# The last tile's up stage as 49 small products instead of 26 larger ones, with their weight sums made in tiles two and three

## The chip, the cores and the metric

The kernel runs on one core of one Trainium2 chip. The metric is the device time in microseconds (us) of one execution, the median over several. A core has five engines that run at once, each through its own list of instructions in order, and that wait for each other by semaphores: TensorE (PE in the profile; PEld is its weight load), VectorE (DVE), ScalarE (ACT), GpSimd (POOL) and SyncE (SP), which here only issues transfers. TensorE writes to PSUM banks, which VectorE and ScalarE read out; the working memory is SBUF. DMA transfers are issued from SP, ACT and POOL queues and run on 16 DMA engines. In a row such as `SPq`, `ACTq` or `PEq` the letter q marks the engine's sequencer: an issue of a transfer or a wait.

## The reference, cut to what matters

```python
# attention (8 batches, 8 heads, 576 positions, 64 wide), a retention without softmax
scores = scale * np.matmul(q, k.transpose(0, 1, 3, 2))
ret = scores * Dmat          # Dmat[i, j] = gamma_h ** (i - j) for i >= j, else 0
attn = np.matmul(ret, v)
x = attn.transpose(0, 2, 1, 3).reshape(4608, 512)
# gated feed-forward: 512 -> 1536 -> 512
g = x @ w_gate
silu = g * (1.0 / (1.0 + np.exp(-g)))
out = (silu * (x @ w_val)) @ w_out
```

All inputs and outputs are float32 (the weights come as float64 and are rounded in the kernel).

## The kernel before, in words

The 4608 tokens are worked on in five tiles: tile 0 has 512 tokens and plain products, tiles 1 to 4 have 1024 each. A tile of 1024 has an **up stage** (x times `w_gate` and `w_val`, SiLU, product, result `hid`) and a **down stage** (`hid` times `w_out`). The attention of the tokens that come next is cut into ticks that are merged between the products of both stages; tile 4 has none left. `up_step`, `down_step` and `merge` write the order of all engines by hand (`manual_schedule`), so each engine's list is the order of the Python calls.

A down or up stage does not make the 32 block products of a 4x2 by 2x4 block product but 26, after the tables `UP` and `DOWN`: every product is of a sum of blocks of x (or `hid`) with a sum of blocks of the weights, and the results are sums of products. The hidden width of 1536 is cut into three quarters (`qd`, `NQ` = 3), each with 26 products in the up stage. An up product is four matmuls of 128x128 weights with 256 tokens: gate and value side by side in one bank, two halves of the contraction each. A float32 matmul shows as two records in the profile, so a product has eight. The four banks A, B, C, E are handed out by `bank` in the order in which they came to rest; `reads` empties them: copies on ScalarE (L1058), sums with a bank on VectorE (L1061), sums without a bank on GpSimd (L1061 POOL), into 12 `part` places, and `result` makes the SiLU on ScalarE (L1145) and the product on VectorE or GpSimd (L1148 to L1152). `down_step` stores outputs from `part` places to memory on SP (L1182).

The sums of weights are made once, in tile 1, on GpSimd (`w_sums`, L910 and L1095) with negations on ScalarE (`negated`, L1085). They take turns in five `extra` places, and some are made in place in `w_up`, over weights that no longer serve. Each operand is stored to memory when it is used, on ScalarE's queue (`up_ops`, L1128); a place can be used again only when its store is done. In tiles 2 to 4 the operands come back through a ring of eight places of 768 columns, one fetch on SP (`fetch`, L1022) as each product is done, eight products ahead. The sums of x are made by `x_sums`: eight on VectorE in the last four steps of the down stage before, the others on GpSimd in the first quarter of the up stage.

Three things set the order around the change: SP's list (operand fetches, output stores, attention loads; each waits in turn), ScalarE's list (bank copies, SiLUs, negations and, in tile 1, operand stores), and VectorE's list (bank sums, products, attention). The lines that move the work:

```python
    turn = [5, 4, 1, 6, 7, 2, 0, 3]                    # L1015: ring place of fetch m is turn[m % 8]
    nc.sync.dma_start(out=ring[:, turn[m % 8], 0 : src.shape[-1]], in_=src)      # L1022
    nc.scalar.dma_start(out=up_ops[qd][i].rearrange("p (g x) -> p g x", g=2), in_=w)   # L1128, tile 1
    at = 2 * (i - (N - 1 - X_FIRST // 2))              # down_step: x sums of the next tile, steps 21 to 24
```

The last three lines of the table `DOWN` matter at the hand-over to tile 4: they end in `out 1 0 ... out 2 9`, in `out 6 2` and in `add 4 b 4, out 0 4`, where the second number of an `out` is the part that is stored. The first lines of `UP` copy their banks into parts 0 and 1, then 2 and 3, then 4 and 5.

## Time and profile before

| what | value |
|---|---|
| median of 3 runs | 1043.55 us (1042.9 to 1045.37) |
| profiled execution, first to last instruction (its span) | 1037.2 us; no other time of this execution is given |
| median of the runs less that span | 6.35 us |
| mean granted TensorE clock | 0.998 |
| tile 1, up and down | 173 to 318, 318 to 400 us |
| tile 2, up and down | 400 to 545, 545 to 621 us |
| tile 3, up and down | 621 to 762, 762 to 831.5 us |
| tile 4, up and down | 831.5 to 966.2, 966.2 to 1037.2 us |
| DMA traffic | 199.12 MB, mean 192 GB/s |
| operand fetch, up (256 KB) and down (384 KB) | 2.6 and 3.8 us from issue to landing |
| operand store, up (256 KB, ScalarE's queue) | 3.7 us from issue to landing |

How to read it: the page gives each engine's busy time as a share of the span, the chain of work that ended last, and groups of instructions by line with tile names (`rest`, `arena`, `x_odd` and `io` are large SBUF tiles that hold several things; `rest` holds the parts). A row "A <- B: total, times, longest" is idle time of A that ended when B was done. A windows row gives, for a stretch of time, the busy us of TensorE, weight load, VectorE, ScalarE and GpSimd, the granted clock, the busy share of the 16 DMA engines, and GB/s. A timeline row gives start, duration, engine, line, operation, output and input, and in brackets how long the engine had been idle and what ended it.

### The profile page before, as it was taken

What the parts mean: (1) busy time and instruction counts of PE and PEld (TensorE: products, weight loads), DVE (VectorE), ACT (ScalarE), POOL (GpSimd) and SP (SyncE); (2) the same over time, 40 slices, a digit from 0 to 9 for tenths busy, and PEclk for the clock granted to TensorE, in tenths of its full rate; (3) what the DMA queues carried; (4) which work ended last, traced back from release to release, by engine and by line L of the source; (5) the groups of instructions that cost most, each with busy time, mean ns of one, the idle gap of its engine ahead of it and who ended that gap; (6) DMA issues with size and microseconds to landing.
All of it is one profiled execution on the core that took longest, in us unless ns stands there. A gap on an engine that the chain in (4) does not pass through costs nothing.

```text
span 1037.2 us, 21564 instructions
## 1 busy us (share of the span) xinstructions
PE 1023.1 (99%) x8440; PEld 846.0 (82%) x8440; DVE 633.2 (61%) x1070; ACT 299.6 (29%) x653; POOL 419.9 (40%) x369
## 2 busy tenths in 40 slices
PE   6999999999999999999999999999999999999998
PEld 5654555888888888888888888888888888888887
DVE  4488878676768667446458685435465644344644
ACT  3566433253544222222322103223211022231110
POOL 3401265867564236522134057222242583222425
PEclk9999999999999999999999999999999999999999
DMA  9999877777679887674686686555554465555653
GB/s 240 258 279 263 200 218 269 204 205 191 196 194 265 211 244 220 177 197 133 188 231 173 176 208 208 153 142 153 159 171 148 143 196 153 153 153 160 182 163 100
DMA packets 307244, 199.12 MB, mean 192 GB/s; under 512 B 215944, under 2 KB 251784, under 8 KB 307144
## 3 DMA queue, kind: packets, MB, share of 16 engines
q1 hardware_dynamic: 275720, 161.17, 58.2%
q10 hardware_dynamic: 30784, 36.18, 10.4%
q8 instruction: 67, 1.10, 0.5%
q0 software_dynamic: 640, 0.39, 0.2%
q14 instruction: 33, 0.27, 0.1%
HBM read 157.58 MB, written 40.11 MB: 191 GB/s over the span
## 4 chain that ended last, share of the span: by engine, by line
PE 93%; DMA 3%; DVE 1%; ACT 1%; issue 1%; SPq 1%; POOL 0%; DVEq 0%; ACTq 0%; POOLq 0%
PE bankC L1124 13%; PE bankE L1124 13%; PE bankB L1124 13%; PE bankA L1124 13%; PE bankB L1173 7%; PE bankC L1173 7%; PE bankE L1173 7%; PE bankA L1173 7%; PE outer L556 2%; PE bankA L877 2%; PE bankB L877 1%; PE bankE L877 1%; PE outer L583 1%; PE inner L597 1%; PE inner L567 1%; PE bankC L877 1%
## 5 line engine op out<-in xcount | busy, mean ns | idle before, releaser
L1061 POOL TENSOR_TENSOR rest<-rest 128x512 f32<-128x512 f32 x65 | 91.7, 1415 | 234.3 <-DVE rest L1061 212.8
L1145 ACT ACTIVATE io<-rest 128x256 f32<-128x256 f32 x180 | 75.0, 416 | 305.4 <-DVE rest L1061 262.4
L1124 PE MATMUL bankC<-rest,arena 128*128 128x256 f32 x544 | 129.0, 380 | 0.0
L1124 PE MATMUL bankA<-rest,arena 128*128 128x256 f32 x544 | 128.7, 379 | 0.0
L910 POOL TENSOR_TENSOR arena<-arena 128x512 f32<-128x512 f32 (+1 forms) x72 | 110.6, 1549 | 37.3 <-DMA up<-arena 26.5
L1124 PE MATMUL bankB<-rest,arena 128*128 128x256 f32 x512 | 121.2, 380 | 0.5 <-DMA arena<-up 0.5
L1124 PE MATMUL bankE<-rest,arena 128*128 128x256 f32 x512 | 121.4, 380 | 0.1
L1152 POOL TENSOR_TENSOR arena<-rest,io 128x256 f32<-128x256 f32 x72 | 51.9, 726 | 167.7 <-ACT io L1145 167.7
L1124 PEld LDWEIGHTS bankA<-rest,arena 128*128 128x128 f32 x544 | 103.2, 190 | 14.5 <-issue 0.5
L1124 PEld LDWEIGHTS bankC<-rest,arena 128*128 128x128 f32 x544 | 102.9, 190 | 14.4 <-POOL arena L910 0.3
L1124 PEld LDWEIGHTS bankB<-rest,arena 128*128 128x128 f32 x512 | 97.0, 190 | 14.0 <-issue 0.8
L1124 PEld LDWEIGHTS bankE<-rest,arena 128*128 128x128 f32 x512 | 97.0, 190 | 13.7 <-DVE rest L1061 0.5
L910 POOL TENSOR_TENSOR rest<-rest 128x256 f32<-128x256 f32 (+1 forms) x69 | 68.9, 1020 | 71.8 <-DMA dn<-rest 35.3
L1061 DVE TENSOR_TENSOR rest<-bankB,rest 128x512 f32<-128x512 f32 x72 | 48.9, 687 | 67.1 <-PE bankB L1124 52.5
L1061 DVE TENSOR_TENSOR rest<-bankC,rest 128x512 f32<-128x512 f32 x72 | 48.9, 687 | 65.5 <-PE bankC L1124 46.9
L1061 DVE TENSOR_TENSOR rest<-bankA,rest 128x512 f32<-128x512 f32 x72 | 48.9, 687 | 61.2 <-PE bankA L1124 45.1
L1061 DVE TENSOR_TENSOR rest<-bankE,rest 128x512 f32<-128x512 f32 x71 | 48.2, 687 | 60.5 <-PE bankE L1124 47.1
L1148 DVE SCALAR_TENSOR_TENSOR arena<-rest,io 128x256 f32<-128x256 f32 x84 | 56.7, 676 | 10.8 <-ACT io L1145 10.8
L1173 PE MATMUL bankC<-arena 128*128 128x256 f32 x252 | 58.3, 380 | 0.1
L1173 PE MATMUL bankB<-arena 128*128 128x256 f32 x252 | 58.2, 381 | 0.0
L1173 PE MATMUL bankA<-arena 128*128 128x256 f32 x252 | 57.9, 379 | 0.0
L1173 PE MATMUL bankE<-arena 128*128 128x256 f32 x252 | 57.9, 379 | 0.0
(204 smaller groups left out, 1626.1 us busy)
## 6 DMA issues: line engine op xcount, KB each, us to landing
arena<-up SPq DMA_DIRECT2D x234, 256.0 KB, 2.6
arena<-dn SPq DMA_DIRECT2D x104, 384.0 KB, 3.8
up<-arena ACTq DMA_DIRECT2D x78, 256.0 KB, 3.7
dn<-rest SPq DMA_DIRECT2D x78, 128.0 KB, 1.8
out_dram<-rest SPq DMA_DIRECT2D x31, 256.0 KB, 3.9
qk<-in_q_dram SPq DMA_DIRECT2D x108, 72.0 KB, 2.6
qk<-in_k_dram SPq DMA_DIRECT2D x108, 72.0 KB, 2.7
rest<-in_moe_w_out_dram ACTq DMA_DIRECT2D x6, 1024.0 KB
```

Source lines behind the costliest of these rows:

```text
L556: m = nc.tensor.matmul(value(i, hl, c), s["v"][rows, at], ret[rows, c % 2 if whole(i) else hl, c // 2], start=start, stop=start, skip_grou ...
L567: nc.tensor.matmul(z[half[hl], r, c], s["kn"][chunk(i, hl, 2 * c + r)], s["v"][rows, at], start=True, stop=True, skip_group_check=True)
L583: nc.tensor.matmul(xr[half[hl]] if c + 1 == NC else value(i, hl, c), state[half[hl], c, :], s["qT"][half[hl], ts(c, L)], start=False, stop ...
L597: nc.tensor.matmul(sc[chunk(i, hl, 2 * c + r)[0], r if whole(i) else hl, c], kT[half[hl], at], qT[half[hl], at], start=True, stop=True, sk ...
L877: nc.tensor.matmul(bank, w, xs[0][:, c, :], start=(c == 0), stop=(c == HP - 1))
L910: eng.tensor_tensor(out=dst, in0=srcs[0], in1=srcs[1], op=ALU.add if op[0] == "add" else ALU.subtract)
L1061: eng.tensor_tensor(out=at(op[1]), in0=at(op[2]), in1=at(op[3]), op=ALU.add if op[0] == "add" else ALU.subtract)
L1124: m = nc.tensor.matmul(b[:, gv * TB : (gv + 1) * TB], w[:, gv, ts(c, P)], rhs[:, c, :], start=(opens and gv == 0 and c == 0), stop=(c == 1 ...
L1145: nc.scalar.activation(out=s, in_=src[:, 0:TB], func=AF.Silu, scale=-1.0 if negative else 1.0)
L1148: return lambda: nc.vector.scalar_tensor_tensor(out=dst, in0=src[:, TB : 2 * TB], scalar=-1.0, in1=s, op0=ALU.mult, op1=ALU.mult)
L1152: nc.gpsimd.tensor_tensor(out=dst, in0=src[:, TB : 2 * TB], in1=s, op=ALU.mult)
L1173: nc.tensor.matmul(b[:, m * TB : (m + 1) * TB], lhs[:, qd, ts(m, P)], w[:, qd], start=(opens and qd == 0 and m == 0), stop=(qd == NQ - 1), ...
```

## The change

In tile 4 (`FINE`) the up stage is replaced by `fine_up`: for each quarter a form with seven products (a 2x2 by 2x2 block product) is applied twice, 49 products for each quarter. A product contracts 128 instead of 2 x 128 and is two matmuls. Seven outer sets (in the order 1, 2, 6, 7, 4, 5, 3) hold seven inner products each. Inner sums are partly made by adding up in a bank: product 1 opens a bank, 6, 7 and 4 add to it, and ScalarE copies the bank between them; 5 and then 3 share another, 2 has its own. VectorE makes the other inner sums and all outer ones, in four held parts, eight temporary ones and four kept places.

The weight operands of this form need other sums. In tile 1 the raw weights of each quarter are stored to memory (`w_raw`), twice 1 MB, at the quarter's first step. Six weight rounds, three in tile 2's up stage and three in tile 3's, load 1 MB of them back into the third quarter's place of `hid`, which is free then, make twelve sums and store seven operand sets (`fine_ops`), on ScalarE's queue. Tile 4 fetches one outer set (917 KB) at a time into three places. Fetches have places of two sizes, and the down operands of tiles 3 and 4 take other ring places. The x sums of tile 4 are made by VectorE in steps 17 to 20 of tile 3's down stage, by GpSimd in steps 21 to 24 and in the first two outer sets.

```diff
+FINE = (4,)
+FINE_ORDER = (1, 2, 6, 7, 4, 5, 3)
+FINE_SETS = {1: 0, 2: 1, 7: 2, 3: 3, 5: 4, 6: 5, 4: 6}
...
+    w_raw = [[dr.tile([P, 2048], F32, name=f"raw{qd}_{g}") for g in range(2)] for qd in range(NQ)]
+    fine_ops = [dr.tile([P, 2 * 7 * 896], F32, name=f"fine{qd}") for qd in range(NQ)]
...
-    fetches = [("dn", 1, i) for i in range(N)]
-    for n in range(2, NTILE):
-        fetches += [("up", qd, i) for qd in range(NQ) for i in range(N)] + [("dn", n, i) for i in range(N)]
-    fetched = [0]
+    fetches = []
+    def queued(what, a, i, slot=None):
+        if what == "fine":
+            lo, width = len([f for f in fetches if f[0] == "fine"]) % 3 * 1792, 1792
+        else:
+            lo = 768 * (turn[len(fetches) % 8] if slot is None else slot)
+            width = 512 if what == "up" else 768
+        fetches.append((what, a, i, lo, width))
+    for n in range(1, NTILE):
+        if n in FINE:
+            for qd in range(NQ):
+                for o in FINE_ORDER:
+                    queued("fine", qd, FINE_SETS[o])
+        elif n > 1:
+            for qd in range(NQ):
+                for i in range(N):
+                    queued("up", qd, i)
+        for i in range(N):
+            if n in FINE:
+                queued("dn", n, i, (i + 7) % 8)
+            else:
+                queued("dn", n, i, (i + 6) % 8 if n + 1 in FINE else None)
+    fetched, used = [0], [0]
...
+        while fetched[0] < len(fetches):
+            lo, width = fetches[fetched[0]][3:]
+            if any(f[3] < lo + width and lo < f[3] + f[4] for f in fetches[used[0] : fetched[0]]):
+                return
+            fetch_one()
...
+        if busy and i == 0:
+            for g in range(2):
+                nc.scalar.dma_start(out=w_raw[qd][g], in_=w_up[:, qd, g].rearrange("p h k x -> p (h k x)"))
+        if n > 1:
+            for f in rounds.pop((n, qd, i), ()):
+                f()
...
+        if n + 1 in FINE:
+            for f in fine_early.pop((n + 1, i), ()):
+                f()
+        elif 0 <= at < X_FIRST and n + 1 < NTILE:
...
+    def weight_round(qd, g, engines):
...
+        fresh4 = [hid[:, 2].rearrange("p h t x -> p (h t x)")[:, 3584:4096].rearrange("p (n y) -> p n y", n=2),
+                  rest[:, last_at : last_at + 512].rearrange("p (n y) -> p n y", n=2),
+                  operands.rearrange("p (s y) -> p s y", y=768)[:, 0:2, 512:768]]
+        fresh3 = raw_flat[:, 0:1152].rearrange("p (s i x) -> p s i x", s=3, i=3)
...
+        def begin():
+            nc.sync.dma_start(out=raw_flat, in_=w_raw[qd][g])
+        def first():
+            combine(e0, t1, quarter(1, 0), quarter(0, 0), -1)
+            combine(e0, quarter(1, 0), quarter(1, 1), quarter(1, 0), -1)
+        def second():
+            combine(e0, t2, quarter(1, 1), t1, -1)
+            combine(e0, t4, quarter(0, 1), t2, -1)
+        def inner(eng, z, new):
+            return [lambda: (combine(eng, new(0), z(0, 1), z(0, 0), -1), combine(eng, z(0, 1), z(1, 1), z(0, 1), -1)),
+                    lambda: (combine(eng, new(1), z(1, 1), new(0), -1), combine(eng, new(2), z(1, 0), new(1), -1))]
+        def store4():
+            for n in range(2):
+                for k in range(2):
+                    nc.scalar.dma_start(out=to[:, 2 * n + k, 0:512].rearrange("p (m x) -> p m x", m=2), in_=quarter(n, k))
+            for i in range(3):
+                for n in range(2):
+                    nc.scalar.dma_start(out=to[:, 2 * n : 2 * n + 2, 512 + i * P : 512 + (i + 1) * P],
+                                        in_=fresh4[i][:, n].rearrange("p (k x) -> p k x", k=2))
+        def store3():
+            nc.scalar.dma_start(out=to[:, 4:7, 0:512], in_=mid.rearrange("p (s x) -> p s x", s=3))
+            nc.scalar.dma_start(out=to[:, 4:7, 512:896], in_=raw_flat[:, 0:1152].rearrange("p (s x) -> p s x", s=3))
+        return [begin, None, first, second, *inner(e1, z4, lambda i: fresh4[i].rearrange("p n (k x) -> p n k x", k=2)), None, store4, None,
+                *inner(e2, z3, lambda i: fresh3[:, :, i]), None, store3]
+    def plan_rounds():
+        V, G = nc.vector, nc.gpsimd
+        order = [(qd, g) for qd in range(NQ) for g in range(2)]
+        at = [(2, 0, 8), (2, 1, 0), (2, 1, 13), (3, 0, 8), (3, 1, 0), (3, 1, 13)]
+        for (qd, g), (n, stage, i) in zip(order, at, strict=True):
+            for d, f in enumerate(weight_round(qd, g, (V, G, V) if stage else (V, V, V))):
+                if f is not None:
+                    rounds.setdefault((n, stage, i + d), []).append(f)
...
+        def outer_sums(eng):
+            return [lambda: combine(eng, sets[5], sets[7], sets[4], 1),
+                    lambda: combine(eng, sets[6], sets[5], sets[1], -1),
+                    lambda: combine(eng, sets[7], sets[1], sets[7], -1),
+                    lambda: combine(eng, sets[3], sets[2], sets[6], -1)]
+        def inner_sums(o, eng):
+            a, (s1, s2, s4) = sets[o], inner[o]
+            return [lambda: combine(eng, s1, a[:, 0, 1], a[:, 1, 1], 1),
+                    lambda: combine(eng, s2, s1, a[:, 0, 0], -1),
+                    lambda: combine(eng, a[:, 0, 1], a[:, 0, 0], a[:, 0, 1], -1),
+                    lambda: combine(eng, s4, a[:, 1, 0], s2, -1)]
...
+        late = [f for o in FINE_ORDER[3:] for f in inner_sums(o, nc.gpsimd)]
+        held = part[0:4]
+        spot = {11: 0, 12: 1, 21: 2, 22: 3}
+        final = {2: (0, 0), 3: (0, 1), 4: (1, 0), 5: (1, 1)}
+        def temps(k):
+            return dict(zip(("p1", "p5", "u2", "u3"), part[4 + 4 * (k % 2) : 8 + 4 * (k % 2)]))
...
+        home = {11: "p1", 12: "u2", 22: "p5", 21: "u3"}
+        def bank_of(k, i):
+            if i in (1, 6, 7, 4):
+                return banks[k % 2]
+            return banks[2 + (k + (i == 2)) % 2]
+        def product(k, i):
+            qd, o = seq[k]
+            _, _, _, lo, width = fetches[base + k]
+            w = operands[:, lo : lo + width].rearrange("p (g i x) -> p g i x", g=2, i=7)[:, :, PLACE[i]]
+            b = bank_of(k, i)
+            opens = i in (1, 2, 5)
+            for g in range(2):
+                nc.tensor.matmul(b[:, g * TB : (g + 1) * TB], w[:, g], x(o, i),
+                                 start=(opens and g == 0), stop=True, skip_group_check=True)
+        def finish(k, c):
+            qd, o = seq[k]
+            (T, H), (t, h) = final[o], divmod(c - 11, 10)
+            src = temps(k)[home[c]]
+            s = io[:, (silus[0] % 4) * TB : (silus[0] % 4 + 1) * TB]
+            silus[0] += 1
+            nc.scalar.activation(out=s, in_=src[:, 0:TB], func=AF.Silu)
+            nc.gpsimd.tensor_tensor(out=hid[:, qd, 2 * H + h, 2 * T + t], in0=src[:, TB : 2 * TB], in1=s, op=ALU.mult)
+        def outer(k, c, src):
+            o = seq[k][1]
+            r, at = held[spot[c]], temps(k)[home[c]]
+            if o == 2 or o == 3:
+                combine(nc.vector, at, src, r, 1)
+            elif o == 6:
+                combine(nc.vector, r, src, r, 1)
+            elif o == 7:
+                combine(nc.vector, kept(k, c), src, r, 1)
+            elif o == 4:
+                combine(nc.vector, at, src, kept(k, c), 1)
+            elif o == 5:
+                combine(nc.vector, r, src, r, 1)
+                combine(nc.vector, at, src, kept(k, c), 1)
+        def made(k, c, a, b):
+            o = seq[k][1]
+            to = held[spot[c]] if o == 1 else temps(k)[home[c]]
+            combine(nc.vector, to, a, b, 1)
+            if o != 1:
+                outer(k, c, to)
+        def done(k, c):
+            if 0 <= k < K and seq[k][1] in final:
+                finish(k, c)
+        def step(k, r):
+            own, last = 0 <= k < K, 0 < k
+            t = temps(k)
+            if own and r == 0:
+                product(k, 1)
+                nc.scalar.copy(out=t["p1"], in_=bank_of(k, 1))
+            if own and r == 1:
+                product(k, 5)
+                nc.scalar.copy(out=t["p5"], in_=bank_of(k, 5))
+            if last and r == 2:
+                product(k - 1, 4)
+                used[0] += 1
+                fetch()
+            if own and r == 3:
+                product(k, 6)
+                nc.scalar.copy(out=t["u2"], in_=bank_of(k, 6))
+            if own and r == 4:
+                product(k, 2)
+            if own and r == 5:
+                product(k, 3)
+            if own and r == 6:
+                product(k, 7)
+                nc.scalar.copy(out=t["u3"], in_=bank_of(k, 7))
+            if late and own:
+                for _ in range(2):
+                    if late:
+                        late.pop(0)()
+            if r == 0 and last:
+                done(k - 1, 12)
+            if r == 1 and last:
+                before = temps(k - 1)
+                made(k - 1, 22, before["u3"], before["p5"])
+                done(k - 1, 22)
+            if r == 2 and last:
+                if seq[k - 1][1] == 1:
+                    nc.scalar.copy(out=held[spot[21]], in_=bank_of(k - 1, 4))
+                else:
+                    outer(k - 1, 21, bank_of(k - 1, 4))
+            if r == 3 and last:
+                done(k - 1, 21)
+            if own and r == 4:
+                made(k, 11, bank_of(k, 2), t["p1"])
+            if own and r == 5:
+                made(k, 12, bank_of(k, 3), t["u2"])
+            if own and r == 6:
+                done(k, 11)
+        return [lambda k=k, r=r: step(k, r) for k in range(K) for r in range(7)] + [lambda r=r: step(K, r) for r in range(4)]
-        ups = [lambda qd=qd, i=i: up_step(n, qd, i) for qd in range(NQ) for i in range(N)]
+        ups = fine_up(n) if n in FINE else [lambda qd=qd, i=i: up_step(n, qd, i) for qd in range(NQ) for i in range(N)]
```

## The prediction

> **What bounds the kernel now.** I read the busy shares and the chain first, then the stages, then what stands around the places that the change touches.
>
> ```profile
> PE 1023.1 (99%) x8440; PEld 846.0 (82%) x8440; DVE 633.2 (61%) x1070; ACT 299.6 (29%) x653; POOL 419.9 (40%) x369
> PE 93%; DMA 3%; DVE 1%; ACT 1%; issue 1%; SPq 1%; POOL 0%; DVEq 0%; ACTq 0%; POOLq 0%
> ```
>
> TensorE is the bound, and from 10 us on nearly nothing else is. So fewer matmul records are worth their time, and every wait that reaches TensorE is lost whole. The windows by stage (TensorE, weight load, VectorE, ScalarE, GpSimd busy, clock, DMA share, GB/s) are the up stages of tiles 1, 2, 3 and 4, then a stretch of tile 2 and two short ones that show what the DMA engines reach:
>
> ```profile
> 173.00:318.00 145.00, 144.88 (x1228) 126.09 (x1227) 103.29 (x172) 61.86 (x136) 96.58 (x73) 1.00 0.74 207
> 400.00:545.00 145.00, 144.54 (x1169) 126.71 (x1164) 75.93 (x145) 39.31 (x87) 49.61 (x49) 1.00 0.67 188
> 621.00:762.00 141.00, 141.00 (x1002) 124.19 (x996) 69.35 (x119) 36.97 (x81) 52.83 (x51) 1.00 0.59 169
> 831.50:966.20 134.70, 134.70 (x626) 118.58 (x625) 56.83 (x88) 34.41 (x74) 49.69 (x49) 1.00 0.59 165
> ...
> 431.00:476.00 45.00, 45.00 (x460) 39.50 (x459) 21.66 (x42) 13.43 (x30) 9.07 (x11) 1.00 0.60 166
> 333.50:338.50 5.00, 5.00 (x25) 4.41 (x24) 4.06 (x6) 1.34 (x4) 0.00 (x0) 1.00 1.02 367
> ```
>
> Tile 4's up stage is TensorE without a gap: 134.7 us for 26 x 3 products of eight records, 0.216 us a record, 1.727 us a product ("step" below). In 333.5 to 338.5 us all 16 DMA engines are full at 367 GB/s. The SP queue of tile 2 and the chain after it show how far the operand ring carries:
>
> ```profile
> 402.36 10.68 SPq L1022 DMA_DIRECT2D arena<-up  x7
> 414.91 1.96 SPq L306 DMA_DIRECT2D qk<-in_q_dram  x4
> 416.91 3.08 SPq L306 DMA_DIRECT2D qk<-in_k_dram  x4
> ...
> 422.86 6.42 SPq L1022 DMA_DIRECT2D arena<-up  x9
> ```
> ```profile
> 422.86 3.97 DMA arena<-up
> 426.83 0.14 issue
> 426.97 1.97 PE bankB L1124 x8
> ```
>
> SP stopped fetching operands from 413.0 to 422.9 us while attention loads stood ahead; the next operand landed at 426.8, and TensorE waited 0.5 us for it. About 10 us without a fetch is all that the eight ring places carry. Last, tile 1's waits on its own stores, and the hand-over from tile 3's down stage to tile 4:
>
> ```profile
> POOL arena L910 <- DMA up<-arena: 26.5, 10, 8.1
> ACT arena L1085 <- DMA up<-arena: 16.5, 10, 2.6
> ```
> ```profile
> 833.53 0.68 DVE L1061 TENSOR_TENSOR rest<-bankC,rest 128x512 f32<-128x512 f32 x1
> 834.23 0.37 SPq L1182 DMA_DIRECT2D out_dram<-rest  x1
> 837.03 1.07 ACT L1058 COPY rest<-bankB 128x512 f32<-128x512 f32 x2 [0.25 <-DMA out_dram<-rest]
> ```
>
> The last output of tile 3's down stage is stored from part 4; the store is issued at 834.23 and a copy into part 4 can only start at 837.03, 5.5 us into tile 4.
>
> **The change, part by part.** The sum is made against the profiled span, 1037.2 us; the median of the runs, 1043.55, is 6.35 us more, and I add that at the end. 0.3% (3.1 us) is about what a measurement of this kernel tells from none.
>
> *TensorE, tile 4.* 147 products of two matmuls, each two records, are 588 records for 624: 36 x 0.216 = 7.8 us less. This is the whole gain.
>
> *Start of tile 4.* The first product's copy now goes to part 4 (before, part 0). Product 6, third in line, waits for it. Nominally it starts 2 x 0.863 us after the stage, at 833.3. The store of part 4 can be issued about 2 us earlier (eight VectorE x sums leave that spot), but SP holds it behind a 0.92 MB operand fetch (0.92/367 = 2.5 us). It lands between 835.2 (issue at 832.4 plus the 2.8 us seen) and 838.5; with a copy of 0.59 us product 6 starts 2.5 to 5.8 us late. I take 5, as the fetch does stand ahead.
>
> *VectorE and ScalarE, tile 4.* VectorE gets 49 sums a quarter, 147 x 0.69 = 101 us of 127. Outer product 5 has 11 of them, and back to back they start 0.61 us apart: 6.8 us in a window of 7 x 0.863 = 6.04. The backlog reaches TensorE through ScalarE, which waits on each SiLU's input with the bank copies behind it: 0 to 1.5 us, three times; I take 0.5 each. At the stage's end product 4 of the last set follows its copy with no product between: 0.16 drain + 0.59 + wake-up, 1 us. Tile 4: -7.8 + 5 + 1.5 + 1 = 0, between -5 and +5. Its x sums move too: four VectorE and twelve GpSimd ones into steps 17 to 24 of the down stage (GpSimd idles 4.28 us there), 16 GpSimd ones into its first two sets; they are first needed by the fourth set, so I cost them at nothing, with the start's range as cover.
>
> *Tile 1.* Each quarter's first step puts 2 x 1.05 MB of raw weights into the ScalarE queue ahead of the operand stores. Stores take 262 KB a step, 152 GB/s; with the trace's 207 GB/s the engines have 160 GB/s to spare, so the 2.1 MB (5.7 us at 367) needs 13 us to be worked off. GpSimd and ScalarE already wait for these stores (42 us in all). The store of slot 11 (step 3) lands some 4 to 6 us later; ScalarE negates that slot at step 4 with SiLUs behind it, and TensorE needs the result at step 8. The store normally lands near 8.7 us, the negation 0.63 and a GpSimd sum 1.35 make 10.7, and the need is at 13.8: 3 us of slack. 0 to 5 us a quarter, I take 2.5, 7.5 in all.
>
> *A weight round* (six; three in tile 2's up stage, three in tile 3's, from steps 8 of quarter 0, 0 and 13 of quarter 1, over 13 steps each). Per round: one 1.05 MB load on SP; 12 sums of 128x512 or 128x384, all VectorE's in quarter 0, and eight VectorE's (0.6 to 1.1 us) and four GpSimd's (1.35) in quarter 1; 12 stores of 3.21 MB on ScalarE's queue, whose issue takes 0.32 to 0.55 each there, ten of them in one step, 4.5 us in which ScalarE copies no bank.
> The load lands 2.9 us (at 367 GB/s) and about 1.6 us of fixed time after its issue; VectorE asks two steps (3.45 us) on, so it stands about 1 us, then carries 5.5 to 8 us of sums over four to eight steps. The last sums overwrite the raw quarters, so they wait for the first MB of stores: ready at about 13.5 us, and at what a tile-2 stretch leaves (367 - 166 = 201 GB/s) 5.2 us, plus 1.6: 20.3 against VectorE's arrival at 15.6. Behind the waiting sum stand the bank sums; TensorE reuses a bank three or four products later, so about 3.5 to 5.2 us of a VectorE stop are free. Cost of a first or second round: 0 to 5 us, I take 2.5 (lag and ScalarE's 4.5 us come on top of the stop).
> *The third round* starts one step after the second ends. Its load goes into the place that the second's last store is still reading. That store (1.34 MB, issued near 22.5 us from the second round's start, behind the rest of 1.79 MB) ends near 22.5 + 6.7 + 1.6 = 30.8; the load stood first on SP at 22.5. So SP, and behind the load every operand fetch, is held 8.3 us, close to the 10 that the ring carries. The load lands at 35.3; VectorE asked at step 15, 25.9: 9.4 us, less 5.2 of banks, plus the two sums ahead of the bank (1.3) and the bank's own 0.69: 6.2 us of TensorE, and the attention step that falls on the same place (VectorE 13.4 of 16 us busy after it) lengthens the way back: 8. Ends: 2 (stores at the full 367) and 13 (no bank slack, operands late too).
> Tile 2: 2.5 + 2.5 + 8 = 13. Tile 3: 12, as its traffic is 20 GB/s less.
>
> *DMA in all.* Over the second and third round: 8.5 MB of rounds and 166 GB/s x 45 us = 7.5 MB, 356 GB/s against 367. By the row it just fits; with the 305 GB/s of 330 to 340 us it would be 52.4 us for 45, 7 us more, inside the third round's 13.
>
> The Trainium skill's page "DMA: Bandwidth & Descriptors" (Where 436 GB/s comes from) puts the limit between HBM and SBUF at about 358 GB/s for a core. The row above, 367 over 5 us, stands a little over that; by the page the two rounds would need 44.7 of 45 us, so page and row give the same close fit. The page speaks against the change in another section (Issuing engines are not separate DMA queues): giving the stores to ScalarE's queue buys no bandwidth.
>
> *Sum.* 0 + 7.5 + 13 + 12 = +32.5: span 1069.7, time 1076.
>
> **The rivals.**
> *All hidden (faster).* One mechanism decides: the third round's load released in time. If its wait and the stores drain so fast that VectorE stands under 5.2 us, banks cover it; the first two rounds and tile 1 are under their slack, and -7.8 + 2.5 to 5 at the start + 1 is left: about 1040. For: TensorE missed only 0.5 us in 145 with 10 us of SP gone. Against: 1.34 MB must end in 4.1 us, 327 GB/s beside 166 of other traffic. It turns when the waits in tiles 1 to 3 sum under some 3 us.
> *Small loss.* Bank slack and ring hold except in the third rounds at 2 to 4 us each, tile 1 hidden: +6 to +16, about 1054.
> *VectorE bounds tile 4.* Of its 147 sums 63 read a bank and 84 SBUF alone. Those SBUF sums took 682 to 697 ns where GpSimd was idle, 1129 in the mean of a group that ran beside it. All at 1.1: 63 x 0.69 + 84 x 1.1 = 136 us, 9 us over TensorE: 1085. Against: GpSimd has only 48 products of 0.72 us and 16 short sums in 127 us.
> The page "SBUF — State Buffer" (SBUF: two separate sides) calls the port pair shared by the two an exclusive lock for a whole instruction. If every one of those 48 us of GpSimd fell on a VectorE sum, an estimate by that rule is 101 + 48 = 149 us, 22 over TensorE; the rows with GpSimd two thirds busy (a 128x256 product 805 ns, against 589 in tile 4) show a third more, not a full block.
> *DMA saturates everything.* Stores at 305 GB/s, tile 1 at 5 us a quarter, third rounds at 13, the others at 5: +15 + 26 + 20 + 5 = +66, 1109.
>
> **How the numbers follow.** The sum as worked out 0.50; the two larger cases 0.16 together; small loss 0.22; all hidden 0.08; nothing measurable 0.04. The likeliest's own range is 1063 to 1092. Leaving out all hidden and the top of the largest, the 8 in 10 range is 1046 to 1104. Slower by over 0.3% 0.88, within 0.04, faster 0.08.
>
> **What would show it.** The up stage of tile 4 near 127 to 137 us, with a ScalarE copy in its first 8 us waiting on an output store; VectorE waits on the raw load of 1 us in the first rounds and 6 to 12 us in the third ones, with SP standing on the last weight store; TensorE gaps there; slot sums of tile 1 waiting longer on stores at each quarter's start. I am wrong if the third load is released before 27 us of the second round's start, or if TensorE's idle time in tiles 2 and 3 stays under 3 us.

## The result and the profile after

The changed kernel takes 1110.85 us (median of 4 runs, 1106.28 to 1113.6) where the kernel before, run beside it, takes 1043.22: a ratio of 1.065, 95% interval 1.062 to 1.0681. The direction of the forecast was right and its size was not: +32.5 us were forecast and +67.6 came, 6.85 us above the upper end of the range. Of one kernel below, with the raw loads early, the profiled run took 1548.71 us at a mean clock of 0.654 where its other three took 1116.6 to 1121.88; its time is that of the three, and its profile is read only for who waits for whom.

First the page of the changed kernel, its busy line and its chain:

```profile
PE 1040.9 (94%) x8404; PEld 850.4 (76%) x8404; DVE 724.1 (65%) x1182; ACT 328.5 (30%) x713; POOL 456.7 (41%) x412
...
PE 55%; DVE 8%; DMA 6%; POOL 2%; issue 2%; ACT 1%; SPq 1%; ACTq 0%; DVEq 0%; POOLq 0%
```

The 36 matmul records less are there (8404 for 8440), yet TensorE is busy 17.8 us longer, and its share of the chain falls from 93% to 55%. The windows of the up stages of tiles 1 to 4 (span, then busy time of TensorE, weight load, VectorE, ScalarE, GpSimd, the granted clock, DMA share, GB/s):

```profile
178.50:331.40 152.90, 148.50 (x1238) 128.77 (x1237) 107.60 (x176) 61.58 (x138) 96.13 (x73) 0.99 0.83 245
411.20:591.00 179.80, 156.26 (x1169) 133.08 (x1170) 96.03 (x172) 38.67 (x87) 61.09 (x58) 0.92 0.74 222
668.10:824.30 156.20, 146.36 (x897) 126.39 (x898) 91.32 (x145) 36.34 (x81) 64.04 (x59) 0.96 0.71 223
893.40:1039.30 145.90, 130.94 (x590) 111.95 (x589) 104.06 (x145) 65.08 (x132) 55.73 (x69) 0.96 0.44 142
```

Before, the four stages took 146.7, 145.2, 139.6 and 134.7 us, from the first product of each to the first of the next stage (the windows shown before the result end up to 2.6 us away from these borders). So tile 1 lost 6.2 us, tile 2 34.6, tile 3 16.6, tile 4 11.2, and 1.5 more in its down stage; the other down stages are as before, and TensorE came to tile 1 4.6 us later, which varies from run to run (173 to 179 us in the profiles below). These make up the 74.7 us between the two profiled spans, 1111.9 and 1037.2. No stage has its DMA engines full on average (shares of 0.44 to 0.83), though short stretches do: 1.04 from 450 to 455 us, while the first round's stores run. The clock is no longer 1.00 everywhere: in tile 2 it is 0.92 on average, and TensorE's busy time there, 156.26 us for 1169 records, was 144.54 before for as many.

Tile 2's first round on the timeline (start, duration, engine, line, operation, and in brackets the idle time before it and what ended it):

```profile
425.70 1.96 SPq L310 DMA_DIRECT2D qk<-in_q_dram  x4
...
433.02 0.55 SPq L321 DMA_DIRECT2D v<-in_v_dram  x1
...
434.13 0.43 SPq L1269 DMA_DIRECT2D arena<-raw  x1
...
440.52 1.42 DVE L1250 TENSOR_TENSOR arena<-arena 128x512 f32<-128x512 f32 x2 [11.13 <-DMA arena<-raw]
...
445.63 3.75 PE L1166 MATMUL bankC<-rest,arena 128*128 128x256 f32 x8 [6.61 <-DVE rest L1097]
449.18 2.54 PE L1166 MATMUL bankA<-rest,arena 128*128 128x256 f32 x8
451.55 1.89 PE L1166 MATMUL bankB<-rest,arena 128*128 128x256 f32 x8
```

The raw load (L1269) stands behind 8.4 us of attention loads (and one operand fetch) on SP, and VectorE can start 6.4 us after its issue. VectorE, which asks for it two steps after its place in the order, stands 11.1 us with the bank sums behind it, and TensorE 6.6. Then come the rows that the forecast had no term for: the next two products take 3.75 and 2.54 us where 1.89 is the rule. The second round goes the same way (7.3 us of attention loads, VectorE stands 12.8 us, TensorE 7.1). The third round of tile 3, with what SP, VectorE and TensorE show:

```profile
751.67 0.32 SPq L1269 DMA_DIRECT2D arena<-raw  x1
...
756.71 1.42 DVE L1250 TENSOR_TENSOR arena<-arena 128x512 f32<-128x512 f32 x2 [5.83 <-DMA arena<-raw]
...
758.79 3.78 PE L1166 MATMUL bankA<-x_odd,arena 128*128 128x256 f32 x8 [4.38 <-DVE rest L1097]
```

The waits that the rounds add, as totals (in all, times, longest):

```profile
DVE arena L1250 <- DMA arena<-raw: 37.9, 6, 12.8
ACT io L1187 <- DMA fine<-arena: 19.1, 3, 6.7
SPq L1053 <- DMA fine<-arena: 17.9, 11, 3.3
SPq L1269 <- DMA fine<-arena: 13.1, 2, 7.8
```

The first is the one forecast. The second, with two more such waits that end on `fine<-rest`, is ScalarE issuing ten stores in one step (5.8 to 7.7 us in which it empties no bank). The last two are SP standing on stores that ScalarE issued; only the last of them was forecast. At last the start of tile 4:

```profile
896.29 0.53 SPq L1053 DMA_DIRECT2D arena<-fine  x1
896.91 1.08 SPq L1224 DMA_DIRECT2D out_dram<-rest  x2
...
904.01 0.59 ACT L1435 COPY rest<-bankA 128x512 f32<-128x512 f32 x1 [22.84 <-DMA out_dram<-rest]
...
904.65 2.08 PE L1389 MATMUL bankA<-rest,arena 128*128 128x256 f32 x4 [8.17 <-ACT rest L1435]
906.52 1.70 PE L1389 MATMUL bankE<-rest,arena 128*128 128x256 f32 x4
908.05 1.03 PE L1389 MATMUL bankC<-rest,arena 128*128 128x256 f32 x4
```

The first copy of the stage waits on the output store out of part 4, which SP issued behind the operand fetch, and TensorE stands 8.2 us; two slow products follow here too.

### The profile page after: what moved, and what is told of

It reads as the page before. It is cut to its first block, busy times and chain, and to the rows that moved or that the text cites. A ratio compares the mean times of both kernels' runs of the same rounds, so it can differ in the third digit from the quotient of the medians.

```text
span 1111.9 us, 21722 instructions
## 1 busy us (share of the span) xinstructions
PE 1040.9 (94%) x8404; PEld 850.4 (76%) x8404; DVE 724.1 (65%) x1182; ACT 328.5 (30%) x713; POOL 456.7 (41%) x412
## 4 chain that ended last, share of the span: by engine, by line
PE 55%; DVE 8%; DMA 6%; POOL 2%; issue 2%; ACT 1%; SPq 1%; ACTq 0%; DVEq 0%; POOLq 0%
PE bankC L1215 6%; PE bankA L1215 6%; PE bankE L1215 6%; PE bankC L1166 6%; PE bankB L1215 5%; PE bankA L1166 5%; PE bankE L1166 5%; PE bankB L1166 5%; DVE rest L1250 3%; PE bankA L1389 3%; PE bankB L1389 3%; DMA arena<-raw 2%; DMA fine<-arena 2%; DVE arena L1250 2%; PE bankE L1389 2%
## 5 line engine op out<-in xcount | busy, mean ns | idle before, releaser
L1187 ACT ACTIVATE io<-rest 128x256 f32<-128x256 f32 x135 | 55.1, 415 | 269.0 <-DVE rest L1097 179.8
L914 POOL TENSOR_TENSOR arena<-arena 128x512 f32<-128x512 f32 (+1 forms) x72 | 110.9, 1552 | 50.2 <-DMA up<-arena 39.2
L1166 PE MATMUL bankC<-rest,arena 128*128 128x256 f32 x392 | 97.6, 394 | 9.4 <-DVE rest L1097 7.1
L1166 PE MATMUL bankA<-rest,arena 128*128 128x256 f32 x376 | 95.1, 398 | 10.3 <-DVE rest L1097 7.1
L1166 PE MATMUL bankE<-rest,arena 128*128 128x256 f32 x360 | 89.1, 392 | 12.0 <-DVE rest L1097 9.6
L1166 PEld LDWEIGHTS bankC<-rest,arena 128*128 128x128 f32 x392 | 76.8, 198 | 22.5 <-issue 10.1
L1166 PEld LDWEIGHTS bankA<-rest,arena 128*128 128x128 f32 x376 | 74.6, 200 | 23.4 <-DVE rest L1097 7.9
L1166 PE MATMUL bankB<-rest,arena 128*128 128x256 f32 x360 | 86.6, 384 | 1.6 <-DVE rest L1097 1.2
L1166 PEld LDWEIGHTS bankE<-rest,arena 128*128 128x128 f32 x360 | 69.9, 196 | 23.6 <-DVE rest L1097 10.8
L1194 POOL TENSOR_TENSOR arena<-rest,io 128x256 f32<-128x256 f32 x48 | 34.8, 732 | 125.3 <-ACT io L1187 125.3
L1166 PEld LDWEIGHTS bankB<-rest,arena 128*128 128x128 f32 x360 | 68.8, 192 | 12.3 <-DVE rest L1097 1.6
L1250 DVE TENSOR_TENSOR arena<-arena 128x512 f32<-128x512 f32 (+1 forms) x52 | 39.5, 766 | 42.7 <-DMA arena<-raw 37.9
L1250 DVE TENSOR_TENSOR rest<-rest 128x512 f32<-128x512 f32 (+1 forms) x67 | 55.4, 842 | 4.3 <-ACT rest L1452 2.7
```

The costliest lines, as they stand in the source:

```text
L914: eng.tensor_tensor(out=dst, in0=srcs[0], in1=srcs[1], op=ALU.add if op[0] == "add" else ALU.subtract)
L1166: m = nc.tensor.matmul(b[:, gv * TB : (gv + 1) * TB], w[:, gv, ts(c, P)], rhs[:, c, :], start=(opens and gv == 0 and c == 0), stop=(c == 1 ...
L1187: nc.scalar.activation(out=s, in_=src[:, 0:TB], func=AF.Silu, scale=-1.0 if negative else 1.0)
L1194: nc.gpsimd.tensor_tensor(out=dst, in0=src[:, TB : 2 * TB], in1=s, op=ALU.mult)
L1250: eng.tensor_tensor(out=out, in0=a, in1=b, op=ALU.add if sign > 0 else ALU.subtract)
```

## The experiments

The theories, as the expectations name them: **A**, the forecast's own (VectorE stands on a late raw load, with the bank sums behind it); **B**, ScalarE's bank copies come late behind its store issues; **C**, the DMA engines are full; **D**, SP's operand loads are held by ScalarE's list; **E**, GpSimd becomes what is waited for, where it gets the work; **F**, the rounds' work is too much wherever it stands; **H**, half clock after a long stop. Times of up stages in us, with TensorE's stops in brackets where they matter:

| kernel | time | ratio to before, 95% | tile 1 | tile 2 | tile 3 | tile 4 |
|---|---|---|---|---|---|---|
| before | 1043.22 | | 146.7 | 145.2 | 139.6 | 134.7 |
| changed | 1110.85 | 1.062 to 1.0681 | 152.9 | 179.8 (23.5) | 156.2 (9.8) | 145.9 (15.0) |
| no rounds | 1063.49, one run | | 152.8 | 145.0 | 139.6 | 146.9 |
| tile 4's form alone | 1053.48 | 1.0085 to 1.0146 | 146.8 | 144.8 | 139.6 | 145.5 (14.4) |
| the same, other parts first | 1046.92 | 1.0032 to 1.0075 | 146.9 | 145.2 | 139.6 | 138.6 (8.7) |
| raw loads early | 1118.73 | 1.07 to 1.079 | | | | |
| stores only | 1089.71 | 1.0385 to 1.0539 | 152.3 | 176.2 (24.1) | 140.5 (0.7) | 146.7 |
| no stores | 1089.55 | 1.0411 to 1.0509 | 153.4 | 168.2 (17.1) | 149.7 (6.1) | 146.6 |
| rounds 16 steps apart | 1114.68 | 1.0645 to 1.0758 | 152.4 | 173.6 (19.8) | 165.9 (17.5) | 147.3 |
| stores only, GpSimd's queue | 1074.14 | 1.0285 to 1.0356 | 150.8 | 155.1 (6.7) | 143.8 (3.7) | 145.9 |
| stores on GpSimd's queue | 1120.83 | 1.073 to 1.0807 | 153.0 | 186.4 (28.4) | 160.7 (14.2) | 146.0 |
| stores and loads there | 1113.31 | 1.0642 to 1.0752 | 153.0 | 174.9 (18.9) | 166.5 (20.1) | 147.3 |
| and 16 apart, other parts | 1116.92 | 1.0667 to 1.0765 | 152.3 | 180.4 (23.4) | 169.2 (19.8) | 139.8 |
| stretched rounds | 1090.68 | 1.0426 to 1.0508 | 154.7 | 176.6 (24.6) | 146.4 (4.5) | 139.9 |
| and loads on GpSimd's queue | 1092.12 | 1.0439 to 1.0542 | 152.4 | 177.1 (22.9) | 146.5 (5.4) | 138.2 |
| and stores on GpSimd's queue | 1096.69 | 1.0484 to 1.0579 | 150.8 | 169.0 (16.1) | 161.2 (13.1) | 138.7 |

**What each part of the change costs.** First the rounds were left out, with tile 4 taking its weights from another input, then the raw stores of tile 1 too:

```diff
-    plan_rounds()
-            src = fine_ops[a].rearrange(...)
+            src = q[a]...
```
```diff
-        if busy and i == 0:
-            for g in range(2):
-                nc.scalar.dma_start(out=w_raw[qd][g], in_=...)
```

> The changed kernel without the six weight rounds: no loads of raw weights, no sums, no stores of operand sets; tile 4 fetches sets of the same size from the input q instead, so its products are not of the right weights. The raw weights are still stored in tile 1. All theories: tiles 2 and 3's up stages return to 145 and 140 us, 51 us less, about 1060 us. If more than 5 us stay in tiles 2 and 3, something other than the rounds (the other ring order, for one) costs there.

> As the run without rounds, and the raw weights are not stored in tile 1 either: only tile 4's own new form and its x sums are left, on operand sets taken from the input q. Tile 1's up stage returns from 152.9 to about 147 us. If tile 4's up stage stays at 146 us and the down stage at 72.7, the total is about 1056 us, and tile 4's form costs 12 us more than it saves, where the prediction had it at 0. If the 4.9 us that tile 0 took more belong to the change and are not chance, about 1061.

Without rounds, tiles 2 and 3 are at 145.0 and 139.6 us, as before: the rounds cost the whole of their loss. Without the raw stores tile 1 goes from 152.8 to 146.8 us: they cost 6.0. Tile 4's form alone is slower than what it replaces, by a ratio of 1.0116.

**Tile 4's start.** The first set was given the temporary parts 10, 11, 8 and 9, where no late output store reads:

```diff
-            return dict(zip(("p1", "p5", "u2", "u3"), part[4 + 4 * (k % 2) : 8 + 4 * (k % 2)]))
+            return dict(zip(("p1", "p5", "u2", "u3"), part[4:8] if k % 2 else part[10:12] + part[8:10]))
```

> As the run with tile 4's form alone, with one difference: the sets 0, 2, 4 ... take parts 10, 11, 8 and 9 as temporary places instead of 4, 5, 6 and 7 in turn, so that the first copy of tile 4 doesn't wait for the output store out of part 4. Theory A (that store is the stop of 8.2 us at the start of tile 4, with some 3 us of half clock behind it): tile 4's up stage falls from 146 to 134 or 135 us, the total to about 1045. Rival (the copy is held by something else, the operand fetch or GpSimd's x sums): the stop stays at 5 us or more.

The first stop falls from 7.6 to 1.9 us, the stage from 145.5 to 138.6 (A had it at 134 or 135) and the time by 6.6 us. So the wait on part 4 was the largest single loss of tile 4. What is left still loses, ratio 1.0053 (1.0032 to 1.0075): stops of 1.40 and 0.48 us behind each quarter's outer product 5 stay. In the changed kernel's rows for the first of these, two of VectorE's sums without a bank take 1.94 us together, 1.22 of them the second, which has a product of GpSimd beside it:

```profile
943.19 1.94 DVE L1250 TENSOR_TENSOR rest<-rest 128x512 f32<-128x512 f32 x2
943.86 0.72 POOL L1401 TENSOR_TENSOR arena<-rest,io 128x256 f32<-128x256 f32 x1 [1.86 <-ACT io L1400]
...
945.89 0.42 ACT L1400 ACTIVATE io<-rest 128x256 f32<-128x256 f32 x1 [1.63 <-DVE rest L1250]
946.22 0.57 ACT L1445 COPY rest<-bankA 128x512 f32<-128x512 f32 x1
946.84 1.13 PE L1389 MATMUL bankA<-x_odd,arena 128*128 128x256 f32 x4 [1.39 <-ACT rest L1445]
```

ScalarE waits on VectorE for a SiLU's input, its bank copy stands behind the SiLU, and TensorE behind the copy. The slower sums are no exception: over the whole changed kernel, VectorE's 128x512 sums that read a bank took 0.69 us with or without GpSimd at work beside them, the 112 without a bank 0.69 us where GpSimd made nothing, and the 79 beside an instruction of GpSimd 1.08 us in the mean, 1.76 at most.

**The raw load earlier.** The loads of each tile's first two rounds were issued five and two steps ahead of their places:

```diff
+                    where = (n, stage, i + d)
+                    if d == 0 and i < 13:
+                        where = (n, 0, 24 if stage else 3)
```

> The changed kernel with one difference: the raw weights of the first and second rounds are loaded earlier (at step 3 of quarter 0 instead of step 8, and at step 24 of quarter 0 instead of step 0 of quarter 1), so that in tile 2 they stand ahead of the attention loads on SP and not behind them; sums and stores stay where they are. Theory A (the rounds cost time because VectorE stands on a load that is late on SP, and TensorE runs at half clock after each long stop): VectorE's two waits of 11.1 and 12.8 us on the raw loads of tile 2 fall under 3 us, the two TensorE stops of 6.6 and 7.1 us and their slow stretches go, tile 2's up stage falls from 179.8 to about 158 us, in all about 1089 us. Rival B (VectorE's own sums and ScalarE's store issues make the stops, whatever the load does): tile 2's up stage stays above 172. Rival C (DMA traffic as a whole is too much): nothing changes by more than 5 us, as the same bytes move.

It became slower, 1118.73 us, which none of the three theories had, though VectorE no longer waits on raw loads in its profile:

```profile
607.68 16.83 SPq L318 DMA_DIRECT2D v<-in_v_dram  x2
...
630.72 3.75 PE L1166 MATMUL bankB<-rest,arena 128*128 128x256 f32 x8 [11.98 <-DMA arena<-up]
```

SP stands 16 us on stores of the fine weights between two loads of `v`, a tile that the stores never touch, and TensorE runs out of operands. So another wait stands where the one removed had been. The next two kernels take the rounds apart.

**Stores alone, and loads and sums alone.**

```diff
-        return [begin, None, first, second, *inner(e1, ...), None, store4, None, *inner(e2, ...), None, store3]
+        return [None] * 7 + [store4, None, None, None, None, store3]                                            # stores only
+        return [begin, None, first, second, *inner(e1, ...), None, None, None, *inner(e2, ...), None, None]     # no stores
```

> The six rounds issue only their twelve stores each (at the same two steps); the loads and the sums are left out, and tile 4 takes its weights from another input, so its results are not the reference's. Without rounds at all the time was 1063.5 us and the up stages of tiles 2 and 3 took 145.0 and 139.6 us. Theory A (VectorE stands on a late raw load and TensorE with it): no raw load, no stop; both up stages within 2 us of those, 1063 to 1067. Theory B (ScalarE, issuing ten stores in one step for 6.6 to 7.7 us, brings the bank copies late): stops of 1 to 3 us behind each ten stores, six times, 1070 to 1080. Theory C or D (stores fill the DMA engines, or hold the operand and attention loads on SP): operands late by several us with SP standing on stores of the fine weights, 1080 or more.

> The six rounds load and sum as in the changed kernel, but store nothing; tile 4 takes its weights from another input, so its results are not the reference's. Theory A with the places that the trace shows (the raw loads of tile 2's first two rounds stand behind attention loads on SP whatever the stores do; the third round's load is held by stores): stops of 6 to 7 us twice in tile 2's up stage with about 3.5 us of half clock each, hence 160 to 165 us for it; tile 3's up stage 140 to 147 us; in all 1080 to 1090. Theory D (the load is late because the stores before it hold SP): little is left, up stages within 3 us of those without rounds, 1063 to 1069.

Each half alone costs tile 2 most of what both cost: 31.2 us for the stores and 23.2 for loads and sums (over 145.0), 34.8 together. They claim the same stretch of time, and taking one away uncovers the other. Loads and sums were not taken apart from each other. In tile 3, which the stores alone leave at 140.5 us, loads and sums cost 10.1 and both 16.6. For "no stores" the rows are those of the first round again, raw load behind attention loads:

```profile
429.45 0.43 SPq L1269 DMA_DIRECT2D arena<-raw  x1
...
436.38 1.42 DVE L1250 TENSOR_TENSOR arena<-arena 128x512 f32<-128x512 f32 x2 [11.98 <-DMA arena<-raw]
...
441.50 3.65 PE L1166 MATMUL bankC<-rest,arena 128*128 128x256 f32 x8 [7.13 <-DVE rest L1097]
```

So A holds, with the load late for a reason that has nothing to do with the stores. For "stores only":

```profile
429.81 8.38 SPq L318 DMA_DIRECT2D v<-in_v_dram  x2
...
435.64 2.00 ACTq L1286 DMA_DIRECT2D fine<-arena  x4
...
439.04 12.43 SPq L1053 DMA_DIRECT2D arena<-up  x11
...
443.34 3.75 PE L1166 MATMUL bankB<-rest,arena 128*128 128x256 f32 x8 [8.52 <-DMA arena<-up]
```

SP waits from 430.2 on for ScalarE's first store, which ScalarE issues only at 435.64, behind a SiLU. The windows of this stretch and of the one behind it (the last two columns are the DMA share and GB/s):

```profile
432.00:436.00 4.00, 2.81 (x14) 2.12 (x12) 1.47 (x3) 0.78 (x2) 0.73 (x2) 1.00 0.00 0
437.00:443.00 6.00, 0.00 (x0) 0.00 (x0) 0.00 (x0) 0.00 (x0) 0.00 (x0) 0.58 1.05 300
```

Until 436 us nothing is saturated: SP waits for a transfer that has not been issued. From 437 us on the stores fill the engines, and the operand fetch issued at 439.04 lands 4.3 us later, where 2.6 is the median in the kernel before; so C has a share in the tail of the stop, of some 1.7 us by this difference. The completion semaphore of each issue, read from the trace, tells why SP waited (start, queue, semaphore, line):

```
428.89 Sync   107 L318        435.64 Scalar 103 L1286
429.81 Sync   101 L318        437.68 Scalar 102 L1289
437.83 Sync   103 L318        438.62 Scalar 104 L1289
438.24 Sync   105 L321        441.43 Scalar 103 L1289
```

The transfers of SP and ScalarE take the same eight semaphores, 100 to 107, in turn in the order of the program, and in the trace the issues that wait name the semaphore that their own transfer takes. SP's load with number 103 may be issued only when the transfer that had 103 before it is done, and that is ScalarE's store. Ten stores in one step take all eight, so whatever SP has next waits until ScalarE has come to them. B shows little in this run: the one stop of TensorE in tiles 2 and 3 that an operand did not end is 0.7 us long.

**The same stores from GpSimd's queue**, whose transfers take semaphores 111 to 118:

```diff
-                    nc.scalar.dma_start(out=to[...], in_=quarter(n, k))
+                    nc.gpsimd.dma_start(out=to[...], in_=quarter(n, k))
```

> The stores of the rounds alone, as in the run with stores only, but issued on GpSimd's queue at the same steps, with the same bytes; loads and sums are left out and tile 4 takes its weights from another input, so its results are not the reference's. Theory D (the operand loads on SP stand behind ScalarE's list: both queues' transfers take the same eight completion semaphores in turn, 100 to 107, and each issue waits for the one that had its semaphore before; GpSimd's transfers use 111 to 118): the three operand stops of tile 2's up stage, 8.5, 9.2 and 6.5 us, go, its length falls from 176 to 145 to 150 us, and the time from 1089.7 to 1062 to 1068. Theory C (the traffic of the stores delays the operands): the stops stay, 1085 to 1095.

The same bytes at the same steps cost 15.6 us less. The stops of 8.5 and 9.2 us are gone, one of 5.0 stays, and small ones behind VectorE and GpSimd come new. That is D for the two stops that went, with less of a gain than expected (1062 to 1068). The stop that stays ends on an operand fetch at 518.06, in a stretch where the engines are full, so there the traffic, C, is the likelier cause:

```profile
510.00:518.00 8.00, 3.07 (x15) 2.36 (x13) 0.00 (x0) 2.39 (x5) 0.00 (x0) 0.94 1.10 274
```

The Trainium skill's page "DMA: Bandwidth & Descriptors" (Issuing engines are not separate DMA queues) says that issuing from several engines buys no bandwidth and only saves issue time; no run here contradicts the part on bandwidth, but most of the 15.6 us come from a third thing, whose transfer a queue's next issue waits for.

**The whole change with that queue, and other spacings.** Stores on GpSimd's queue; raw loads there too; the rounds 16 steps apart, on the old queues and (with tile 4's other parts) on GpSimd's:

```diff
-        at = [(2, 0, 8), (2, 1, 0), (2, 1, 13), (3, 0, 8), (3, 1, 0), (3, 1, 13)]
+        at = [(n, s) for n in (2, 3) for s in (3, 19, 35)]
```

> The changed kernel with the rounds' stores alone on GpSimd's queue, the raw loads on SP as before. Theory D: the stores' share goes, the loads' share stays (the raw load behind attention loads, stops of 6 to 7 us twice in tile 2): 1080 to 1095 us, slower than with the loads on GpSimd's queue too. Theory C: 1105 to 1115.

> The changed kernel with the rounds' stores and raw loads on GpSimd's queue. Theory D: SP and ScalarE no longer stand on rounds; what is left in tile 2 is what the loads and sums cost alone (17.1 us of stops in the run without stores, and less where the raw load no longer stands behind attention loads); tile 2's up stage 150 to 165 us and tile 3's 140 to 150 us, 1070 to 1092 us. Theory C: 1105 to 1115 as in the changed kernel. Rival E (GpSimd, which stands on the rounds now, becomes the one that the products wait for): stops behind GpSimd's sums and products, 1095 or more.

> The changed kernel with the three rounds of a tile 16 steps apart (from steps 3, 19 and 35 of the 52, where they were 8, 26 and 39). Theory A (the third round's load stands on the second's last stores, since it starts one step behind its end): SP is held 3 us less there, TensorE's stops behind the third rounds fall from 7 to under 3 us, 1098 to 1104 us. Theory A' (it is the attention loads ahead of the raw loads on SP that decide, and the new places meet other attention loads): the stops move but do not go, 1106 to 1118 us.

> Rounds wholly on GpSimd's queue, 16 steps apart (from 3, 19 and 35), and tile 4's first sets with the temporary parts that took 7 us off its start. By the terms found: 1053.5 for tile 4's form alone, 6.6 less for the parts, 6 more for the raw stores of tile 1, and 5 to 20 for what is left of the rounds: 1058 to 1073 us, still slower than the kernel before.

None of the four is faster than the changed kernel. The rounds 16 steps apart met what A' expected, stops that move and do not go; the three with GpSimd's queue missed what was expected. The loads there are no clear gain: VectorE's waits on them sum to 17.9 us in tile 2, for 28.5 with the loads on SP, but to 21.3 in tile 3, for 12.7, and the intervals of the two times, of two runs each, overlap. In the run with stores and loads there, E is a part of what happens:

```profile
441.65 2.96 POOL L1286 DMA_DIRECT2D fine<-arena  x4
444.61 1.44 POOL L1289 DMA_DIRECT2D fine<-arena  x2
...
450.26 0.69 DVE L1097 TENSOR_TENSOR rest<-bankC,rest 128x512 f32<-128x512 f32 x1 [9.21 <-POOL rest L1097]
```

GpSimd issues ten stores at 0.72 us each, its sums stand behind them, and VectorE waits 9.2 us for one of these, once in each of tiles 2 and 3. The larger part is still A: VectorE's waits on the raw loads sum to 39.2 us in the two tiles. The run lies in the range of C too (1105 to 1115), which its time alone can't tell from E.

**Rounds stretched over 16 or 17 steps**: the load four steps ahead of its sums, two stores in a step over five steps, from steps 1, 18 and 35, with tile 4's other parts; then the same with the raw loads, and with the stores, on GpSimd's queue:

```diff
+        return [begin, None, None, None, first, second, *inner(e1, ...),
+                lambda: quarters(0), lambda: quarters(1), lambda: fresh(0), lambda: fresh(1), lambda: fresh(2),
+                *inner(e2, ...), store3]
```

> The whole change, with each round stretched over its 16 or 17 steps: the raw load four steps ahead of the first sums, the ten stores two in a step over five steps, the last two at the end; rounds from steps 1, 18 and 35; tile 4's first sets with the other temporary parts. Theory D with A (each stop came from a queue in which a late piece of a round stood ahead of something else: the raw load behind attention loads with VectorE two steps behind it, ten stores in one step taking all eight shared semaphores): with four steps' lead and two stores a step, tile 2's up stage falls from 180 to 150 to 162 us and tile 3's from 156 to 141 to 148 us, in all 1062 to 1080 us. Theory F (the rounds' work itself is too much wherever it stands, since in-order queues have no place for it): 1100 or more, as with every other placing tried so far.

> The same with the raw loads on GpSimd's queue, where no attention load stands ahead. Theory A: the VectorE waits on raw loads shrink further than in the run beside it, 3 to 10 us less in all; rival E (GpSimd stands on the load's place until the stores before have left it, and its sums come late): 5 to 20 us more than beside it.

> The stretched rounds with their stores on GpSimd's queue, all else as in the stretched run (1090.7 us, with operand stops of 10.7 and 7.7 us in tile 2 while SP stood on attention loads, and 4.5 us of stops in tile 3). Theory D (those two stops are SP waiting, through the shared eight semaphores, for stores that ScalarE has not issued yet; GpSimd's transfers have their own eight): both stops go, tile 2's up stage falls from 176.6 to 147 to 158 us, the time to 1062 to 1074 us. Rival E (GpSimd's sums come late behind its own store issues): new stops on VectorE and GpSimd in tiles 2 and 3 of as much, 1085 us or more.

Stretching takes 20 us back, some 6 of them by tile 4's parts; at 1090.68 it lies between the ranges of D with A and of F. It gave tile 3 back 9.8 of its 16.6 us (146.4 us, 4.5 of stops, VectorE on raw loads 1.5 and 1.8 us), and left tile 2 at 176.6, where it was expected at 150 to 162. There SP stands again, for 6.0 us of the 7.87 on a store of the fine weights:

```profile
429.02 7.87 SPq L310 DMA_DIRECT2D qk<-in_k_dram  x4
...
446.85 3.75 PE L1166 MATMUL bankB<-rest,arena 128*128 128x256 f32 x8 [10.73 <-DMA arena<-up]
```

With the stores on GpSimd's queue those two stops shrink from 10.7 and 7.7 us to 2.5 and 4.6, as D says, and tile 2 by 7.6 us. But tile 3 loses 14.8: VectorE's waits of over 1 us on GpSimd's sums rise from 7.3 to 14.3 us there, as E says, and those on raw loads from 3.3 to 8.5. The whole is no faster: 1.0531 of the kernel before for 1.0467, with intervals that overlap. Loads on GpSimd's queue make no difference that the runs can tell. The stretched version is the best of the whole change that was found, and it is still 4.7% slower than the kernel before. No version here beats that: the parts of the loss are shown by leaving work out, and no run shows the whole change without them.

**The clock.** Six chains of 2 to 14 ScalarE copies were put into tile 4's up stage of the kernel before, with TensorE waiting for each:

```diff
+        if n + 1 == NTILE and (qd, i) in stalls:
+            for c in range(stalls[qd, i]):
+                last = nc.scalar.copy(out=rest[:, ...], in_=...)
+            # TensorE's next product waits for last
```

> The kernel before, with six chains of 2, 3, 4, 6, 9 and 14 ScalarE copies of 128x512 in tile 4's up stage, for each of which TensorE waits: stops of rising length, from about 1 to about 9 us, in a stage that has no other. Theory H (a stop of TensorE of about 2.4 us or more is followed by some 3.4 us at half the clock): after the stops under 2 us the next product takes 1.7 to 1.9 us as ever, after each longer one the next two products together take 3.4 us more than two, the same whatever the stop's length. Rival (what is slow after a stop is the operand or the bank that it waited for, and not the clock): products after these made stops, for which all operands lie ready, take 1.7 to 1.9 us.

The products after the six stops, and some that follow them:

```profile
856.93 1.97 PE L1125 MATMUL bankB<-rest,arena 128*128 128x256 f32 x8 [1.37 <-ACT rest L1130]
858.73 1.89 PE L1125 MATMUL bankE<-rest,arena 128*128 128x256 f32 x8
...
873.00 2.38 PE L1125 MATMUL bankB<-rest,arena 128*128 128x256 f32 x8 [2.02 <-DVE rest L1062]
...
908.68 3.58 PE L1125 MATMUL bankC<-rest,arena 128*128 128x256 f32 x8 [2.67 <-ACT rest L1130]
912.10 1.89 PE L1125 MATMUL bankB<-rest,arena 128*128 128x256 f32 x8
...
928.32 3.06 PE L1125 MATMUL bankC<-rest,arena 128*128 128x256 f32 x8 [3.97 <-issue]
931.18 2.52 PE L1125 MATMUL bankA<-rest,arena 128*128 128x256 f32 x8
...
967.24 3.75 PE L1125 MATMUL bankE<-rest,arena 128*128 128x256 f32 x8 [5.92 <-ACT rest L1130]
...
993.50 3.75 PE L1125 MATMUL bankE<-rest,arena 128*128 128x256 f32 x8 [9.16 <-issue]
```

The stage took 171.1 us for 134.7: 25.1 us of stops and 11.3 us of slow products, for which all operands lay ready. H holds in its main point, since the stop of 1.4 us costs nothing more and the others do. Its threshold of about 2.4 us is too high, as the stop of 2.02 us shows, and its 3.4 us, the same for each, does not hold: the starts of the products that follow are late by 1.7 to 3.1 us in all (1.77, 1.69, 1.76, 3.1 and 1.95 in the order of the stops).

## Why the prediction was wrong

**The step that failed is the cost of a first or second round** ("0 to 5 us, I take 2.5"). It let the raw load be issued at its place in the order and land about 4.5 us later, so that VectorE would stand about 1 us. In tile 2 the load stood behind 8.4 and 7.3 us of attention loads on SP and came 6.4 and 5.7 us after its issue, VectorE stood 11.1 and 12.8 us, and TensorE 6.6 and 7.1, plus the slow products behind each. The term for tile 2 was 13 us, of which 5 for these two rounds; measured were 34.6. In tile 3, where VectorE waited 1.2 and 3.9 us on these loads, the term was about right, as far as the loads go; TensorE's one long stop there, 3.9 us in the first round, came behind VectorE's own sums, which had waited 1.2 us for a SiLU that ScalarE made after the ten stores. The row that would have told it was among the lines shown: the attention loads ahead of the operand fetches, which the working used for the ring's reach and not for the load that the change puts into the same list.

**No term held the two lists together.** The forecast looked at ScalarE's stores as traffic and as 4.5 us of issue time. The runs with stores alone show that they also stop SP, by semaphores in common, and cost tile 2 31 us with no load or sum beside them. That could have been seen before: in the profile before, SP's attention loads (L306) wait in tile 1 on ScalarE's operand stores, with which they share no tile:

```profile
SPq L306 <- DMA up<-arena: 21.8, 12, 3.4
```

**No term held the clock.** Of the 34.6 us in tile 2, 23.5 are stops and 11 are the slower products; of the 16.6 in tile 3, 9.8 and 6.8. Stops were priced by their length alone, which leaves out a third of the loss in tile 2 and more in tile 3.

**The third rounds** were right in kind. SP stood on the second round's store 5.3 us in tile 2 and 7.8 in tile 3 (8.3 forecast), and VectorE then 3.2 and 5.8 us (9.4 forecast). TensorE's stops from the third load on sum to 8.6 us in tile 2, near the 8 of the sum but 3.2 of them on an operand, and to 5.6 in tile 3. The two conditions under which the forecast called itself wrong did not come: the third load was released 29.4 and 30.3 us after the second's, and TensorE's idle time in tiles 2 and 3 was 33 us.

**Tile 4**, 0 forecast between -5 and +5, measured +11.2 in the up stage and +1.5 in the down stage. The mechanism of the start was right and its size was not: 8.2 us for 5, from the same store behind the same fetch. The store was issued 4.2 us into the stage and landed 6.3 us later, where the working took the 2.8 us of the row before. VectorE's backlog behind outer product 5 came three times as forecast, at 1.9 us each for 0.5, because sums without a bank took longer beside GpSimd: 28 of the stage's 82 ran so, at 1.05 us in the mean, and the others took 0.69. So the rival in which VectorE bounds tile 4 was right in its row and wrong in its weight, as it put all of them at 1.1. The x sums, costed at nothing, are the likely cause of the 0.98 us stop at the stage's start, where VectorE waited on a GpSimd sum that stood behind two of them.

**Tile 1** was right in its sum: 7.5 forecast, 6.2 measured in the profile and 6.0 by leaving the raw stores out. It was not made up as forecast, 2.5 in each quarter: TensorE stopped once behind GpSimd's sums (2.4 us) and once behind a bank copy of ScalarE (1.9), so that the sum came so near is in part luck. (The two rows of waits on stores that the working adds up to 42 us make 43.)

**The rivals.** 1109 us for "DMA saturates everything" is nearly the number that came, but for the most part by another mechanism: the engines were at 0.71 to 0.83 of their time in tiles 1 to 3, in the run with stores alone they stood idle while SP waited, and the same stores cost 15.6 us less from another queue. Full engines come in behind such waits, as the rows of the runs with stores alone show. The likeliest case's own range, up to 1092, was left by the two missing terms together.

## What to carry to other kernels

A step that is moved into an in-order queue has to be priced at the place where it will be issued, not where it stands in the program: list what stands ahead of it there, also the work of another stage, and what stands behind the instruction that waits for it. Count how many transfers share the completion semaphores before putting ten into one step, since a queue then waits for another engine's progress with the DMA engines idle. And where TensorE was never idle before, price a stop of 3 us or more at its length plus some 2 to 3 us (1.8 to 3.1 behind the made ones of 4 us and more).
